# Five moves in the hand-written order of engine work of a fused linear-attention and long-convolution kernel

## Chip, cores and metric

One core of a Trainium2 chip runs the whole kernel. The metric is the device time of one execution in microseconds (us). Six agents work at once and meet only at semaphores: PE (TensorE, matrix products), PEld (its weight loads), DVE (VectorE), ACT (ScalarE), POOL (GpSimd) and SP (SyncE, which issues the transfers). Each of them does its own list of instructions strictly in the order in which the program gives them.

## What is computed

The input x has 2048 rows of D = 448. The result is `g * a + (1 - g) * b`, with one gate g for each row:

```python
g = sigmoid((x * gate_w).sum(-1, keepdims=True))
# a: linear attention, 16 heads of 28
pq, pk = phi(q), phi(k)                       # phi(t) = where(t > 0, t + 1, exp(t)) + 1e-6
kv  = einsum("bhsd,bhse->bhde", pk, v)
z   = einsum("bhsd->bhd", pk)
o   = einsum("bhqd,bhde->bhqe", pq, kv) / (einsum("bhqd,bhd->bhq", pq, z)[..., None] + 1e-6)
a   = o @ wo
# b: a causal convolution over the 2048 rows, one kernel K for each of the 448 columns, and a skip
b   = irfft(rfft(u) * rfft(K))[:L] + u * D_skip
```

For the given data the kernel of the convolution is the same at every lag, to the precision of the sum, for each column that passes a test; so the convolution is a running sum over the rows times one number per column (the "taps"), and the kernel holds a general version behind a branch for columns that fail the test.

## The kernel before

The rows are cut into 16 chunks c = 0..15 of 128. Everything lies in one program under a manual schedule: an engine's instructions stand in the order in which the Python code issues them, and buffers are taken in turn from pools with tags, so that a tile which takes a buffer waits until the last reader of its former tile is done. Matrix products run on pairs of reduced-precision numbers (a high part and a low part), so each operand x, w, pk is "split": ACT copies the high part, POOL or DVE subtracts to get the low part (line 261).

There are three stages.

**First stage, chunks 0 to 14.** For each chunk `project` (PE, L353) makes k of the next chunk and q of this one from the transposed input `xt` and the weights `wk`, `wqh`, `wql`; `k_feature`, `k_high`, `k_low` and `q_post` put phi on them (ACT, DVE); `do_g` (L422) adds pk times x into four sums g, which hold the whole of k times v, since v is linear in x. `split_t` and `split_n` split the two layouts of a later chunk (`xt` transposed, `xn` natural); `split_n` ends with the skip product `y <- xr * dsk` on POOL (L273, `dsk` is the second part of the tile `rows`). `do_v` (L429, L430) makes the running sum of a chunk on PE by a triangular matrix `tri`; `v_post` multiplies it by the taps (`near`, the first part of `rows`) on DVE (L434) and POOL adds it to y (L441). The table VS says which v belong to which c: v(0) and v(1) to c = 5. The taps are worked out from the convolution's parameters in small steps between the chunks (`s4d_prepare`, resumed by `steps`): its fifth step makes `tri` (L327) and the tests on DVE, its sixth, at c = 5, has four PE transposes into a tile p (L334) and an ACT copy into `rows` (L335). The tile p and the odd v share the PSUM tag "v1", which has one buffer.

**Transition, chunks 14 and 15.** The sum of all pk (`zb`) goes through PE (zo, L640) and back by an ACT copy (L642). Now for each chunk `norm_a` (POOL, L537) makes `prod = pq * zb`, `norm_b` (DVE reduce, L542) and `norm_d` (DVE, L547, L549) make the reciprocal denominators `den`, `norm_c` makes the normalised `pn` in two POOL products and one DVE product (L560, L566, L563). `norm_bd` is `norm_b` and `norm_d` for one chunk. `prod` has two buffers, so `norm_a` of a chunk waits for `norm_b` of the chunk two before it. Beside this `kv_products` (L694) turns g into kv, `kv_split` masks it (DVE, L699 to L707) and copies its high part `kvh` (ACT, L709), `kv_low` makes `kvl` (DVE), and `mrows` (L684 to L687) multiplies with wo into the four blocks of the last stage's weights `wk` (its low part again on DVE; `shl` is one such block). `turn` (L594 to L599) transposes a pn on PE into `tr`, ACT copies it to `th` and DVE makes the low part.

**Last stage, c = 0..15.** `attend(c)` (L616) is 11 matmuls a <- th, wk. `final_b` (DVE, L621) adds y times its gate and sends the rows out; `final_c` (ACT) keeps a copy. The loop makes pn of chunk c + 3 and turns chunk c + 2 ahead of `attend(c)`; chunks 0 and 1 are turned and pn 0 to 2 made in the transition. The rest of q of chunk 15 (`late`) is done in small pieces in the loop.

Of the kernel before, what the change touches and what calls it, by code (L numbers as in the profile page):

```python
# [11 lines left out]
ALU = mybir.AluOpType  # L12
# [5 lines left out]
D = 448  # L18
# [3 lines left out]
NC = S // P  # L22
# [146 lines left out]
def gated_mix_kernel(ctx: ExitStack, tc: tile.TileContext, xin, wq_d, wv_d, wo_d, abc_d, ldt_d, dsk_d,  # L169
# [6 lines left out]
    y = keep.tile([P, NC, D], F32, name="y")  # L176
# [91 lines left out]
    def split_n(c):  # L268
        r, w = plain[c], xn_p.tile([P, NX], F32R, name="xn", tag="n")
        xn[c] = w  # L270
        ACT.copy(w[:, :XC - NAT], r)  # L271
        low(POOL, w[:, XC - NAT:], r[:, :D], w[:, :D])
        POOL.tensor_tensor(out=y[:, c], in0=r[:, :D], in1=dsk, op=ALU.mult)  # L273

    idle = ps.tile([P, 512], F32, name="q", tag="q")

# [80 lines left out]
    def project(*args, **kw):  # L357
        o, run = pieces(*args, **kw)
        run(11)
        return o  # L360
# [15 lines left out]
    def k_feature(c, o):  # L376
        e = tp.tile([P, D], F32, name="e", tag="e")
        pks[c] = o[:, :D]
        ACT.activation(e, pks[c], AF.Relu, scale=-1.0)  # L379
        ACT.activation(e, e, AF.Exp, scale=-1.0)  # L380
        DVE.scalar_tensor_tensor(out=pks[c], in0=pks[c], scalar=1.0, in1=e, op0=ALU.add, op1=ALU.max)  # L381

    def k_high(c):
        pkh[c] = tp.tile([P, D], F32R, name="pkh", tag="pkh")
        ACT.add(pkh[c], pks[c], 1e-6)  # L385
# [19 lines left out]
    def gate(a, b):  # L405
        DVE.tensor_scalar(out=e1[:, a:b], in0=e1[:, a:b], scalar1=1.0, scalar2=None, op0=ALU.add)
        DVE.reciprocal(out=og[:, a:b], in_=e1[:, a:b])
        DVE.tensor_scalar(out=og[:, a:b], in0=og[:, a:b], scalar1=-1.0, scalar2=1.0, op0=ALU.mult, op1=ALU.add)
# [5 lines left out]
    def do_g(c, blocks=range(4)):  # L414
        w = xn[c]
        for i in blocks:
            a = w[:, 64 + i * P:64 + (i + 1) * P]
            b = w[:, XC - NAT + 64 + i * P:][:, :P] if i < 3 else None
            seq = [(a, pkh[c]), (a, pkl[c]), (b, pkh[c])] if i < 3 else \
                  [(a, pkh[c]), (a[:, :64], pkl[c])][::1 if c == 0 else -1]  # L420
            for n, (a, b) in enumerate(seq):
                PE.matmul(g[i][:a.shape[1], :D], lhsT=a, rhs=b, start=c == 0 and n == 0,  # L422
                          stop=c == NC - 1 and n == len(seq) - 1)
# [8 lines left out]
    def v_post(c):  # L432
        t = tp.tile([P, D], F32, name="t", tag="v0")
        DVE.tensor_tensor(out=t, in0=vt.pop(c)[:, :D], in1=near, op=ALU.mult)  # L434
        if c < NC - 1:
            SP.dma_start(out=u[c:c + 1], in_=t[P - 1:P])
            v_add(c, t)
        return t
# [5 lines left out]
    def steps(n):  # L444
        for _ in range(n):
            next(prep, None)
# [20 lines left out]
    split_n(0)  # L467
    k_low(0)
    k_feature(1, ko[1])
    k_high(1)  # L470
    split_n(1)
    k_low(1)
    do_g(0)
    split_w(1, wqh, wql, wqr, POOL)
# [11 lines left out]
    DVE.memset(ones, 1.0)  # L486
    q_post(1, qo)
    steps(1)
    split_n(3)
    woh, wol = [], []  # L490
    for c in range(2, NC - 2):
        if c + 3 < NC:
            load_x(c + 3)
        if c == 2:
            for o, i in ((mask, mask_d), (gcat, gcat_d), (sel, sel_d)):
                SP.dma_start(out=o, in_=i)
        if c == 4:
            SP.dma_start(out=wv, in_=wv_d)
            SP.dma_start(out=wo, in_=wo_d)
        vs = VS.get(c, ())  # L500
        ko = project(c + 1, wkh, wkl, D, "k")
        if c == 5:
            steps(1)
        for v in vs[:1]:
            do_v(v)
        split_t(c + 2)
        k_feature(c + 1, ko)
        k_high(c + 1)
        for v in vs[:1]:
            v_post(v)  # L510
        k_low(c + 1)
        qo = project(c, wqh, wql, D + 2, "q")
        for v in vs[1:]:
            do_v(v)
        q_post(c, qo)
        for v in vs[1:]:
            v_post(v)
        if c < 5:
            steps(2 if c == 4 else 1)
        do_g(c)  # L520
        split_n(c + 2)
        for j in {11: (0, 1), 12: (2, 3)}.get(c, ()):
            w = xn_p.tile([P, NX], F32R, name="wo", tag="n")[:DJ, :2 * D].rearrange("p (i d) -> p i d", i=2)
            woh.append(w[:, 0])
            wol.append(w[:, 1])
            ACT.copy(woh[j], wo[:, j])
            low(POOL, wol[j], wo[:, j], woh[j])
# [11 lines left out]
    def norm_b(c):  # L539
        if c % 2 == 0:  # L540
            dn[c // 2] = tp.tile([P, 2, H], F32, name="den", tag="den", bufs=3)
        DVE.tensor_reduce(out=dn[c // 2][:, c % 2], in_=pd.pop(c).rearrange("p (h d) -> p h d", h=H), op=ALU.add,  # L542
                          axis=AX.X)
# [7 lines left out]
    def norm_bd(c):  # L551
        norm_b(c)
        norm_d(c, 1)
# [36 lines left out]
    def turn(c):  # L590
        o = p3.tile([P, 512], F32, name="tr", tag="tr")
        n = pn.pop(c)
        for j in range(J):
            PE.transpose(o[:, j * P:(j + 1) * P], n[:, j], ident)  # L594
        t = xt_p.tile([P, 2, J, P], F32R, name="th", tag="t")
        h, l = th[c], tl[c] = t[:, 0], t[:, 1]
        ov = o.rearrange("p (j t) -> p j t", j=J)
        ACT.copy(h, ov)  # L598
        DVE.tensor_tensor(out=l, in0=ov, in1=h.bitcast(F32), op=ALU.subtract)  # L599
# [31 lines left out]
    do_v(c + 1)  # L631
    k_feature(c + 1, ko)
    k_high(c + 1)
    gate(0, c)
    k_low(c + 1)
    vl = v_post(c + 1)
    qo = project(c, wqh, wql, D + 2, "q")
    zo = ps.tile([P, 512], F32, name="zo", tag="v0")
    PE.matmul(zo[:1, D:D + 1], lhsT=ones[:DJ, :1], rhs=oks, start=True, stop=True)
    PE.matmul(zo[:, :D], lhsT=ones, rhs=zb, start=True, stop=True)  # L640
# [1 line left out]
    ACT.copy(zb, zo[:, :D])  # L642
    norm_a(0)
    norm_a(1)
    do_g(c)
    gate(c, c + 1)
    g2 = gates_a(1, NC - 1)
    POOL.memset(rows[DT:RX, :2 * D], 0.0)
    last = gates_b(g2, "pkl")
# [30 lines left out]
    def mrows(j, pool, tag):  # L680
        o = pool.tile([P, 512], F32, name="m%d" % j, tag=tag)
        w = woh[j]
        for n, (a, b) in enumerate(((kvh, w), (kvh, wol[j]), (kvl, w))):
            PE.matmul(o[:DJ, :D], lhsT=a[:, j], rhs=b, start=n == 0, stop=n == 2)  # L684
        a, b = (mh[:DJ, j], ml[:DJ, j]) if j < 3 else (shl[:, 0], shl[:, 1])
        ACT.copy(a, o[:DJ, :D])
        DVE.tensor_tensor(out=b, in0=o[:DJ, :D], in1=a.bitcast(F32), op=ALU.subtract)  # L687
# [9 lines left out]
    def kv_split(r, kvp):  # L697
        m = 3 if r else 2
        DVE.tensor_tensor(out=kv[:, 2 * r:m],  # L699
                          in0=kvp[:DJ, 2 * r * DJ:m * DJ].rearrange("p (j d) -> p j d", d=DJ),  # L700
                          in1=mask[:, None, :].to_broadcast([DJ, m - 2 * r, DJ]), op=ALU.mult)
        if r:
            a, b = (w.rearrange("p (h d) -> p h d", h=4) for w in (kvp[:DJ, 3 * DJ:4 * DJ], mask))
            DVE.tensor_tensor(out=kv[:, 3, :DT].rearrange("p (h d) -> p h d", h=4), in0=a[:, :, DS:], in1=b[:, :, DS:],
                              op=ALU.mult)
            a, b = (w[:, :, :DS].rearrange("p h (j d) -> p h j d", j=3) for w in (a, b))
            DVE.tensor_tensor(out=kv[:, 3, DT:].rearrange("p (j h d) -> p h j d", j=3, h=4), in0=a, in1=b, op=ALU.mult)  # L707
        rs = slice(2 * r, 2 * r + 2)
        ACT.copy(kvh[:, rs], kv[:, rs])  # L709

    def kv_low(r):
        rs = slice(2 * r, 2 * r + 2)
        low(DVE, kvl[:, rs], kv[:, rs], kvh[:, rs])
# [2 lines left out]
    q_run(QA)  # L716
    k1 = kv_products(1)
    k0 = kv_products(0)
    norm_bd(2)
    norm_a(3)  # L720
    kv_split(1, k1)
    kv_low(1)
    kv_split(0, k0)
    mrows(3, ps, "k")
    for j, eng in ((2, SP), (0, ACT), (1, SP)):
        eng.dma_start(out=wk2[DJ:, :, j].bitcast(F32), in_=shl[DT + 16 * j:DT + 16 * j + 16].bitcast(F32))
    SP.dma_start(out=mh[DT:, 3].bitcast(F32), in_=shl[:DT, 1].bitcast(F32))
    kv_low(0)
    mrows(2, ps, "v0")
    turn(0)  # L730
    v_add(c + 1, vl)
    norm_c(2)
    norm_a(4)
    mrows(0, p3, "a")
    ACT.copy(mh[:DT, 3], shl[:DT, 0].bitcast(F32))
    mrows(1, p3, "a")
    ACT.copy(rc[0][:DT], shl[:DT, 0].bitcast(F32))
    turn(1)
    norm_bd(3)
    norm_a(5)  # L740
    tail(0)
    q_run(11)
    norm_b(4)
    def late():
        c = NC - 1
        yield 5
# [21 lines left out]
    for c in range(NC):  # L768
        if c % 2 and c + 4 < NC:
            norm_d(c + 3, 2)  # L770
        if c:
            final_b(c - 1)
        if c + 3 < NC:
            norm_c(c + 3)
        if c + 2 < NC:
            turn(c + 2)
        if c:
            final_c(c - 1)
        if c + 1 < NC:
            tail(c + 1)  # L780
        if c + 6 < NC:
            norm_a(c + 6)
        if c + 5 < NC - 1:
            phi(c + 5)
        attend(c, ((0, D // 2), (D // 2, D)) if c == NC - 1 else ((0, D),))
        if c + 5 < NC:
            norm_b(c + 5)
        if c == due:
            due = next(later, None)
# [94 lines left out]
```

## Time and profile before

| | us |
|---|---|
| median of 3 runs (lowest, highest) | 185.66 (185.36, 185.93) |
| the profiled execution | 185.38 |
| its span in the trace | 183.6 |
| PE busy in the span | 173.2 (94%) |
| PEld, DVE, ACT, POOL busy | 151.4, 112.9, 94.7, 118.8 |

The span reaches from the first to the last instruction in the trace; the other 1.8 us of the execution lie around it. Busy time is the sum of an engine's instruction times without overlap. In the timeline a row has the start and the duration in us, the engine, the line, the operation, what it writes and reads, the number of merged instructions, and in brackets how long the engine had been idle and which instruction let it go on.

### The profile page before, as it was taken

How to read it: one execution, taken by the hardware profiler on the slowest of the kernel's cores; microseconds unless marked ns; L12 is line 12 of the kernel's file. 1: busy time of each engine (PE TensorE's matmuls, PEld its weight loads, DVE VectorE, ACT ScalarE, POOL GpSimd, SP SyncE). 2: the span in 40 equal slices, each digit the busy share in tenths (PEclk: the TensorE clock that was granted, in tenths of full speed). 3: DMA queues.
4: the chain of work that ended last, by engine and by line, in shares of the span. 5: the costliest groups of instructions: out<-in, count | busy, mean ns of one | idle time of the engine just before them, and what ended most of it. 6: DMA issues, size and time to landing. Idle time of an engine off the chain costs nothing.

```text
span 183.6 us, 2736 instructions
## 1 busy us (share of the span) xinstructions
PE 173.2 (94%) x879; PEld 151.4 (82%) x879; DVE 112.9 (62%) x238; ACT 94.7 (52%) x212; POOL 118.8 (65%) x124
## 2 busy tenths in 40 slices
PE   6999999999899999999999999998899999999970
PEld 2697798998899999999989999667678999999970
DVE  1757638558357374372651733788699999987430
ACT  3769288872536245262455742551654565455330
POOL 3259774766268769669599996098548887864000
PEclk9999999999999999999999999999999999999999
DMA  5999966920003303033033000000201221222131
GB/s 196 409 303 274 281 232 232 300 73 2 4 3 112 115 0 116 4 115 115 1 114 118 2 0 0 0 2 5 39 26 50 101 102 53 101 100 85 71 127 39
DMA packets 7789, 18.46 MB, mean 101 GB/s; under 512 B 1755, under 2 KB 4520, under 8 KB 7768
## 3 DMA queue, kind: packets, MB, share of 16 engines
q1 hardware_dynamic: 7720, 18.16, 29.9%
q8 instruction: 9, 0.15, 0.3%
q10 hardware_dynamic: 48, 0.06, 0.2%
q14 instruction: 12, 0.10, 0.2%
HBM read 14.20 MB, written 3.67 MB: 97 GB/s over the span
## 4 chain that ended last, share of the span: by engine, by line
PE 71%; DVE 9%; POOL 6%; issue 6%; ACT 5%; ACTq 0%; POOLq 0%; DVEq 0%
PE a L616 19%; PE k L353 15%; PE q L353 14%; PE g L422 12%; PE tr L594 3%; PE q L279 3%; PE v L430 2%; PE v L429 2%; POOL wql L261 2%; POOL y L273 2%; POOL xn L261 1%; DVE den L542 1%; PE v L353 1%; DVE den L547 1%; POOL prod L537 1%
## 5 line engine op out<-in xcount | busy, mean ns | idle before, releaser
L616 PE MATMUL a<-wk,th 128*128 128x448 f32 (+1 forms) x170 | 39.0, 362 | 0.0
L422 PE MATMUL g<-pkh,xn 128*128 128x448 f32 x112 | 36.0, 370 | 0.2 <-POOL xn L261 0.2
L353 PE MATMUL k<-wk,xt 128*128 128x448 f32 x154 | 34.8, 370 | 0.0
L381 DVE SCALAR_TENSOR_TENSOR k<-k,e 128x448 f32<-128x448 f32 x14 | 8.9, 632 | 40.9 <-ACT e L380 40.9
L353 PEld LDWEIGHTS k<-wk,xt 128*128 128x128 f32 x154 | 28.8, 188 | 3.7 <-ACT wk L450 0.6
L616 PEld LDWEIGHTS a<-wk,th 128*128 128x128 f32 x170 | 29.8, 189 | 2.0
L353 PE MATMUL q<-wqh,xt 128*128 128x450 f32 x120 | 27.8, 369 | 0.0
L441 POOL TENSOR_TENSOR y<-y,t 128x448 f32<-128x448 f32 x16 | 18.5, 1154 | 11.3 <-DVE t L434 11.1
L261 POOL TENSOR_TENSOR xn<-xr,xn 128x448 fp32r<-128x448 f32 x16 | 18.5, 1155 | 10.2 <-ACT xn L271 10.1
L353 PEld LDWEIGHTS q<-wqh,xt 128*128 128x128 f32 x120 | 22.6, 189 | 2.6 <-issue 0.7
L537 POOL TENSOR_TENSOR prod<-pq,zb 128x448 f32<-128x448 f32 x16 | 18.4, 1152 | 9.2 <-ACT zb L642 5.8
L422 PEld LDWEIGHTS g<-pkh,xn 128*128 128x128 f32 x112 | 21.0, 188 | 3.4 <-POOL xn L261 0.6
L422 PE MATMUL g<-pkl,xn 128*128 128x448 f32 x64 | 23.4, 366 | 0.0
L379 ACT ACTIVATE e<-k 128x448 f32<-128x448 f32 x14 | 7.6, 545 | 27.2 <-PE k L353 27.2
L261 POOL TENSOR_TENSOR xt<-xr,xt 128x512 fp32r<-128x512 f32 x14 | 18.1, 1294 | 3.2 <-ACT xt L265 3.2
L273 POOL TENSOR_TENSOR y<-xr,rows 128x448 f32<-128x448 f32 x16 | 18.6, 1161 | 0.8 <-DMA rows<-in 0.8
L560 POOL TENSOR_TENSOR pn<-pq,den 128x336 f32<-128x336 f32 x16 | 12.1, 755 | 8.0 <-PE tr L594 5.2
L598 ACT CAST th<-tr 128x512 fp32r<-128x512 f32 x16 | 9.4, 588 | 14.5 <-PE tr L594 14.4
L621 DVE SCALAR_TENSOR_TENSOR ot<-y,og,a 128x448 f32<-128x448 f32 (+1 forms) x17 | 10.5, 615 | 5.7 <-PE a L616 5.7
L385 ACT ACTIVATE pkh<-k 128x448 fp32r<-128x448 f32 x14 | 7.6, 546 | 9.8 <-DVE k L381 9.8
L353 PE MATMUL q<-wql,xt 128*128 128x450 f32 x45 | 12.0, 367 | 0.4 <-POOL wql L261 0.4
L422 PEld LDWEIGHTS g<-pkl,xn 128*128 128x128 f32 x64 | 11.2, 175 | 1.2 <-issue 0.2
(135 smaller groups left out, 292.3 us busy)
## 6 DMA issues: line engine op xcount, KB each, us to landing
xr<-in SPq DMA_DIRECT2D x15, 512.0 KB, 3.3
out<-ot SPq DMA_DIRECT2D x15, 224.0 KB, 1.9
pq<-in SPq DMA_DIRECT2D x4, 448.0 KB, 12.3
y<-in SPq DMA_DIRECT2D x2, 480.0 KB
y<-in SPq DMA_DIRECT2D x2, 450.0 KB, 7.4
wv<-in SPq DMA_DIRECT2D x1, 896.0 KB, 7.6
wo<-in SPq DMA_DIRECT2D x1, 784.0 KB
y<-in SPq DMA_DIRECT2D x1, 448.0 KB
```

The costliest lines, as they stand in the source:

```text
L261: eng.tensor_tensor(out=o, in0=r, in1=h.bitcast(F32), op=ALU.subtract)
L273: POOL.tensor_tensor(out=y[:, c], in0=r[:, :D], in1=dsk, op=ALU.mult)
L353: PE.matmul(o[:, :n], lhsT=a, rhs=b, start=run.n == 1, stop=not seq)
L379: ACT.activation(e, pks[c], AF.Relu, scale=-1.0)
L381: DVE.scalar_tensor_tensor(out=pks[c], in0=pks[c], scalar=1.0, in1=e, op0=ALU.add, op1=ALU.max)
L422: PE.matmul(g[i][:a.shape[1], :D], lhsT=a, rhs=b, start=c == 0 and n == 0, stop=c == NC - 1 and n == len(seq) - 1)
L441: POOL.tensor_tensor(out=y[:, c], in0=y[:, c], in1=t, op=ALU.add)
L537: POOL.tensor_tensor(out=pd[c], in0=pq[:, c], in1=zb, op=ALU.mult)
L560: POOL.tensor_tensor(out=n[:, :3, :DJ].rearrange("p j (h d) -> p j h d", h=4), in0=a, in1=r[:, :H - 4].rearrange("p (j h) -> p j h", j=3)[ ...
L598: ACT.copy(h, ov)
L616: PE.matmul(a[:, lo:hi], lhsT=u_, rhs=w_[:, lo:hi], start=n == 0, stop=n == 10)
L621: DVE.scalar_tensor_tensor(out=ot[:, lo:hi], in0=y[:, c, lo:hi], scalar=og[:, c:c + 1], in1=a[:, lo:hi], op0=ALU.mult, op1=ALU.add)
```

## The change

Five moves; no instruction of weight is added or taken out. (1) The skip products of chunks 0 to 2 leave `split_n` and are issued together behind q of chunk 1; `split_n(1)` is issued ahead of `k_high(1)`. (2) At c = 5 the step with the four transposes p stands behind q of chunk 5, directly ahead of v(1), and both `v_post` of that chunk behind `q_post`. (3) In the block of chunk 14 the first quarter of `do_g(14)` stands ahead of zo, and one gate calculation over chunks 0 to 14 takes the place of two. (4) `kv_split` and `kv_low` for both halves come ahead of the denominators of chunk 2, which go behind all four `mrows`; turn(1), pn(2) and the denominators of chunks 3 and 4 go into the last loop. (5) The last loop makes pn of c + 2 and turns c + 1.

```diff
 def split_n(c):                                        # (1)
...
     low(POOL, w[:, XC - NAT:], r[:, :D], w[:, :D])
-    POOL.tensor_tensor(out=y[:, c], in0=r[:, :D], in1=dsk, op=ALU.mult)
+    if c > 2:
+        skip(c)
+
+def skip(c):
+    POOL.tensor_tensor(out=y[:, c], in0=plain[c][:, :D], in1=dsk, op=ALU.mult)
...
 k_feature(1, ko[1])
+split_n(1)
 k_high(1)
-split_n(1)
 k_low(1)
...
 q_post(1, qo)
 steps(1)
+for c in range(3):
+    skip(c)
 split_n(3)
...
     ko = project(c + 1, wkh, wkl, D, "k")              # (2)
-    if c == 5:
-        steps(1)
     for v in vs[:1]:
         do_v(v)
...
-    for v in vs[:1]:
-        v_post(v)
+    if c > 5:
+        for v in vs[:1]:
+            v_post(v)
     k_low(c + 1)
     qo = project(c, wqh, wql, D + 2, "q")
+    if c == 5:
+        steps(1)
     for v in vs[1:]:
         do_v(v)
     q_post(c, qo)
-    for v in vs[1:]:
+    for v in vs[c > 5:]:
         v_post(v)
...
-gate(0, c)                                             # (3)
 k_low(c + 1)
 vl = v_post(c + 1)
 qo = project(c, wqh, wql, D + 2, "q")
+do_g(c, (0,))
 zo = ps.tile([P, 512], F32, name="zo", tag="v0")
...
-do_g(c)
-gate(c, c + 1)
+do_g(c, (1, 2, 3))
+gate(0, c + 1)
...
 k0 = kv_products(0)                                    # (4)
-norm_bd(2)
+kv_split(1, k1)
 norm_a(3)
-kv_split(1, k1)
 kv_low(1)
 kv_split(0, k0)
+kv_low(0)
 mrows(3, ps, "k")
...
-kv_low(0)
 mrows(2, ps, "v0")
 turn(0)
 v_add(c + 1, vl)
-norm_c(2)
 norm_a(4)
 mrows(0, p3, "a")
...
 mrows(1, p3, "a")
...
-turn(1)
-norm_bd(3)
+norm_bd(2)
 norm_a(5)
 tail(0)
 q_run(11)
-norm_b(4)
...
 for c in range(NC):                                    # (5)
...
-    if c + 3 < NC:
-        norm_c(c + 3)
     if c + 2 < NC:
-        turn(c + 2)
+        norm_c(c + 2)
+    if c + 1 < NC:
+        turn(c + 1)
...
     attend(c, ((0, D // 2), (D // 2, D)) if c == NC - 1 else ((0, D),))
+    if c == 0:
+        norm_bd(3)
+        norm_b(4)
     if c + 5 < NC:
         norm_b(c + 5)
```

What this moves on POOL in the first chunks, before (xn and xt are the low parts of the two layouts of x, wql the low parts of q's weights, `y<-xr,rows` the skip products):

```order
11 L261 TENSOR_TENSOR xn<-xr,xn 128x448
12 L273 TENSOR_TENSOR y<-xr,rows 128x448
13 L261 TENSOR_TENSOR xn<-xr,xn 128x448
14 L273 TENSOR_TENSOR y<-xr,rows 128x448
15 L261 TENSOR_TENSOR wql<-y,wqh 128x450 x2
16 L261 TENSOR_TENSOR xt<-xr,xt 128x512
17 L261 TENSOR_TENSOR xn<-xr,xn 128x448
18 L273 TENSOR_TENSOR y<-xr,rows 128x448
19 L261 TENSOR_TENSOR xn<-xr,xn 128x448
20 L273 TENSOR_TENSOR y<-xr,rows 128x448
21 L261 TENSOR_TENSOR xt<-xr,xt 128x512
```

And now, on the same engine at the same place:

```order
11 L261 TENSOR_TENSOR xn<-xr,xn 128x448 x2
12 L261 TENSOR_TENSOR wql<-y,wqh 128x450 x2
13 L261 TENSOR_TENSOR xt<-xr,xt 128x512
14 L261 TENSOR_TENSOR xn<-xr,xn 128x448
15 L277 TENSOR_TENSOR y<-xr,rows 128x448 x3
16 L261 TENSOR_TENSOR xn<-xr,xn 128x448
17 L277 TENSOR_TENSOR y<-xr,rows 128x448
18 L261 TENSOR_TENSOR xt<-xr,xt 128x512
```

The low parts of xn(1) and of wql come two skip products sooner; three skip products now stand between xn(2) and xn(3), and so ahead of the low part of xt(4).

What it moves on PE in chunk 5, before (p are the transposes of the taps, v the two running sums, k and q the projections, g the sums of pk times x):

```order
102 L353 MATMUL k<-wk_69,xt 128x448 x11
103 L334 MATMUL p<-ident,sm 128x112 x4
104 L429 MATMUL v<-xn,tri 128x448
105 L430 MATMUL v<-xn,tri 128x448
106 L353 MATMUL q<-wqh,xt 128x450 x8
107 L353 MATMUL q<-wql,xt 128x450 x3
108 L429 MATMUL v<-xn,tri 128x448
109 L430 MATMUL v<-xn,tri 128x448
```

And now:

```order
102 L357 MATMUL k<-wk_69,xt 128x448 x11
103 L433 MATMUL v<-xn,tri 128x448
104 L434 MATMUL v<-xn,tri 128x448
105 L357 MATMUL q<-wqh,xt 128x450 x8
106 L357 MATMUL q<-wql,xt 128x450 x3
107 L338 MATMUL p<-ident,sm 128x112 x4
108 L433 MATMUL v<-xn,tri 128x448
109 L434 MATMUL v<-xn,tri 128x448
```

The four transposes went behind the eleven matmuls of q and stand right ahead of v(1).

What it moves on POOL between the transition and the last stage, before (the first row is pn(1)'s second product; prod, pn as above, `y<-y,t` the sum of chunk 15):

```order
74 L566 TENSOR_TENSOR pn<-pq,den 128x128
75 L537 TENSOR_TENSOR prod<-pq,zb 128x448
76 L441 TENSOR_TENSOR y<-y,t 128x448
77 L560 TENSOR_TENSOR pn<-pq,den 128x3x112
78 L566 TENSOR_TENSOR pn<-pq,den 128x128
79 L537 TENSOR_TENSOR prod<-pq,zb 128x448 x2
80 L560 TENSOR_TENSOR pn<-pq,den 128x3x112
81 L566 TENSOR_TENSOR pn<-pq,den 128x128
```

And now:

```order
71 L573 TENSOR_TENSOR pn<-pq,den 128x128
72 L544 TENSOR_TENSOR prod<-pq,zb 128x448
73 L445 TENSOR_TENSOR y<-y,t 128x448
74 L544 TENSOR_TENSOR prod<-pq,zb 128x448 x2
75 L567 TENSOR_TENSOR pn<-pq,den 128x3x112
76 L573 TENSOR_TENSOR pn<-pq,den 128x128
```

The pair of products pn(2) moved behind prod(4) and prod(5); the pn that stood there before was pn(3).

## The prediction

> **What bounds the kernel now.** I read the page's busy times first, then the chain that ended last, then windows around the places that the change touches, then the timeline there.
>
> ```profile
> PE 173.2 (94%) x879; PEld 151.4 (82%) x879; DVE 112.9 (62%) x238; ACT 94.7 (52%) x212; POOL 118.8 (65%) x124
> PE 71%; DVE 9%; POOL 6%; issue 6%; ACT 5%; ACTq 0%; POOLq 0%; DVEq 0%
> ```
>
> PE bounds it: 173.2 of 183.6 us, and 71% of the chain. The change takes no matmul away, so all it can win is PE's idle time, 10.4 us in the span, and only the part that its five moves touch. Windows of the transition and of the last stage:
>
> ```profile
> 130.00:138.00 8.00, 6.96 (x39) 5.70 (x37) 6.96 (x15) 4.46 (x10) 4.58 (x7) 1.00 0.18 37
> 138.00:162.00 24.00, 23.99 (x134) 21.70 (x133) 23.55 (x52) 13.12 (x29) 20.47 (x29) 1.00 0.23 86
> ```
>
> The columns are PE, PEld, DVE, ACT, POOL busy, then the granted clock. Just ahead of the last stage PE loses 1.04 us in 8.00; in its first 24 us PE loses nothing, but DVE is busy 23.55 of the 24.00, so it has no slack to take a delay. The span is 183.6 and the execution 185.38, 1.8 us lie outside; the median is 185.66. The sum is made as a difference and put on both.
>
> **Move 1, skip products later.** The rows of POOL and PE in the first chunks:
>
> ```profile
> 13.81 1.16 POOL L273 TENSOR_TENSOR y<-xr,rows 128x448 f32<-128x448 f32 x1 [0.78 <-DMA rows<-in]
> 14.93 1.16 POOL L261 TENSOR_TENSOR xn<-xr,xn 128x448 fp32r<-128x448 f32 x1
> 15.59 0.36 PE L422 MATMUL g<-pkl,xn 128*128 128x448 f32 x1
> 16.14 0.67 PE L422 MATMUL g<-pkh,xn 128*128 128x448 f32 x2 [0.19 <-POOL xn L261]
> 17.14 3.05 POOL L261 TENSOR_TENSOR wql<-y,wqh 128x450 fp32r<-128x450 f32 x2
> 19.49 0.36 PE L353 MATMUL q<-wql,xt 128*128 128x450 f32 x1
> 20.25 0.47 PE L353 MATMUL q<-wql,xt 128*128 128x450 f32 x1 [0.40 <-POOL wql L261]
> 22.35 1.16 POOL L261 TENSOR_TENSOR xn<-xr,xn 128x448 fp32r<-128x448 f32 x1 [0.92 <-ACT xn L271]
> 28.15 1.31 POOL L261 TENSOR_TENSOR xt<-xr,xt 128x512 fp32r<-128x512 f32 x1
> 30.00 0.85 PE L353 MATMUL k<-wk,xt 128*128 128x448 f32 x3
> ```
>
> Matmuls of this size start some 0.20 us apart (the two rows of 0.36 end the run that each stands in). From 15.59 to 16.14 is 0.55, so 0.35 is lost to xn(1), whose low part stands behind a skip product that itself waited 0.78 for a transfer; from 19.49 to 20.25 is 0.76, 0.56 lost to wql, behind the second skip product. The two matmuls that resume are each 0.1 longer (0.67 for 0.57, 0.47 for 0.36). Together 1.1 us; with xn(1) and wql moved up by one and two skip products (1.1 and 2.2 us on POOL), both waits go. What is late next: on POOL xn(2) still waits for its ACT copy, now at 22.35 - 1.07 = 21.3; behind it stand three skip products (3 x 1.1), xn(3), its skip product and then xt(4): 21.3 + 6 x 1.11 = 28.0, and xt(4) is done at 28.0 + 1.31 = 29.3, where before it was done at 29.5 against a use at about 30.2, the second matmul of k at 30.00. That use would now come at 29.1, so PE waits 0.15 to 0.45 (0.3 to 0.45 if the resumed matmul is longer again). Left: 0.6, between 0.2 and 1.1. That `split_n(1)` stands ahead of `k_high(1)` makes pkh(1) later by one ACT copy, some 0.6 as the copies below, while PE still has g(0): nothing, and at most 0.6 without that cover, which is in the 0.2.
>
> **Move 2, taps behind q of chunk 5.** The rows there:
>
> ```profile
> 42.70 1.15 POOL L261 TENSOR_TENSOR xn<-xr,xn 128x448 fp32r<-128x448 f32 x1 [0.71 <-ACT xn L271]
> 42.73 1.37 DVE L369 TENSOR_SCALAR t<-e 128x448 f32<-128x448 f32 x1
> 45.99 0.22 DVE L327 CAST tri<-trir 128x128 fp32r<-128x128 f32 x1
> 46.53 0.60 PE L334 MATMUL p<-ident,sm 112*128 112x112 f32 x4 [0.64 <-DVE sm L300]
> 47.16 0.53 ACT L335 COPY rows<-p 128x448 f32<-128x448 f32 x1 [4.54 <-PE p L334]
> 47.39 1.81 PE L353 MATMUL q<-wqh,xt 128*128 128x450 f32 x8
> 49.66 0.37 PE L429 MATMUL v<-xn,tri 128*128 128x448 f32 x1
> ```
>
> PE was idle 0.64 ahead of p at 46.53, counted from the modelled end of k; in a dense run the next matmul starts 0.16 before that end (0.36 long, 0.20 apart), so PE was free near 45.73 and 0.8 is lost, to the last of the small DVE steps. Behind q that wait is gone. But v(0), now first, needs `tri`, done at 46.21, so with all 0.6 earlier PE still waits from 45.13 to 45.6: 0.5. Then v(0) and q take to 48.3, p 0.36 more, and v(1) shares p's PSUM buffer: it must wait for the ACT copy of p, which starts 0.63 after p does (47.16 - 46.53) and lasts 0.53. That puts v(1) at 48.3 + 0.63 + 0.53 + 0.06 = 49.5, against 49.66. The early gain of 0.6 shrinks to 0.14 there: a wait of 0.8 turns into one of 0.5 and one of 0.85, and behind the waiting v(1) stand g(5) and k of the next chunk on PE. The moved `v_post` have POOL's sum behind them, which no one needs before the last stage: nothing. Up: the DVE row of 1.37 us ran beside POOL's xn, which started 0.03 us ahead of it, while the same instruction in the last stage takes 0.38 (quoted below); were it to start first, the chain to `tri` is up to 1 us shorter, the wait for `tri` goes, and 0.6 is left. Range 0 to 0.9 for what is kept by chunk 6. From here to chunk 14 PE is dense, and DVE, POOL and ACT follow it: no change.
>
> **Moves 3 and 4, the transition.** The rows:
>
> ```profile
> 117.44 1.02 PE L640 MATMUL zo<-zb,ones 128*128 128x448 f32 x2 [0.43 <-DVE zb L391]
> 124.21 1.73 PE L694 MATMUL k<-gs,wv 128*112 128x112 f32 x16
> 127.06 0.28 DVE L699 TENSOR_TENSOR kv<-k,mask 112x112 f32<-112x112 f32 x1
> 129.77 0.62 DVE L687 TENSOR_TENSOR shl<-m,shl 112x448 fp32r<-112x448 f32 x1 [1.00 <-ACT shl L686]
> 131.16 0.46 PE L684 MATMUL m<-wo,kvl 112*112 112x448 f32 x1 [0.73 <-DVE kvl L261]
> 133.00 1.16 DVE L687 TENSOR_TENSOR wk<-m,wk 112x448 fp32r<-112x448 f32 x2
> 134.92 1.67 PE L616 MATMUL a<-wk,th 128*128 128x448 f32 x7
> 135.10 0.61 DVE L542 TENSOR_REDUCE den<-prod 128x16 f32<-128x448 f32 x1
> 135.74 0.17 DVE L547 SCALAR_TENSOR_TENSOR den<-den,e 128x16 f32<-128x16 f32 x1
> 135.78 1.16 POOL L537 TENSOR_TENSOR prod<-pq,zb 128x448 f32<-128x448 f32 x1 [3.32 <-DVE den L542]
> 136.90 0.76 POOL L560 TENSOR_TENSOR pn<-pq,den 128x336 f32<-128x336 f32 x1
> 137.71 0.69 PE L594 MATMUL tr<-ident,pn 128*128 128x128 f32 x4 [0.31 <-POOL pn L560]
> 138.15 1.68 PE L616 MATMUL a<-wk,th 128*128 128x448 f32 x7
> 141.04 1.68 PE L616 MATMUL a<-wk,th 128*128 128x448 f32 x7
> ```
>
> The masks run at 127.06, behind the denominators of chunk 2, though k's products end by 124.21 + 1.73 = 125.94. With a quarter of g ahead of zo, PE does not wait for `zb` (0.43, and 0.1 for the resumed matmul); with the 0.14 kept from before, the products end near 125.4, and so do the masks begin. That is 1.6 sooner, and the chain mask, kvh, m, low part of m that ends at 133.00 + 1.16 = 134.16 comes some 1.35 sooner, to about 132.8 (each m takes an ACT copy and a DVE subtraction, so not all 1.6 gets through). PE's own 0.73 at 131.16 goes with it, and the four transfers of `shl` rows, issued behind its low part at 129.77, go out as much sooner. a(0), at 134.92 before, can start near 132.4: 2.5 sooner, with one turn less in front. The single gate calculation saves three DVE instructions that nobody waits for: nothing.
>
> But the next turn needs pn(2), and this is now later in its chain. The denominators of chunk 2 begin behind the low parts, at 132.75; prod(4) needs the buffer that their reduce frees, so it starts at 133.4 and holds up DVE's next steps; then the low part of th(1) (to 135.2), the reduce of chunk 3 (0.6, to 135.8), and only that lets prod(5) go: 135.84 to 137.0, nearly the 135.78 of before. pn(2) stands behind it on POOL, its large product to 137.7. So turn(2) starts at 137.75 where before turn(3) started at 137.71, and a(1) at 138.2 to 138.5 against 138.15. PE idles for some 3 us after a(0), and the 2.5 us are gone. Bounds of this term: +0.35 (138.5), and -0.8 if prod(4) does not block DVE and the lows end 0.4 sooner; I take +0.1.
>
> a(2) follows a(1) by 2.89 before (141.04 - 138.15), 2.69 where nothing waits: -0.18.
>
> **Move 5, one ahead.** Before, the turns of four chunks were done by a(1); now three. The one left over runs in the loop, which PE bounds:
>
> ```profile
> 153.94 0.38 DVE L753 TENSOR_SCALAR t<-e 128x448 f32<-128x448 f32 x1
> 155.01 0.76 POOL L560 TENSOR_TENSOR pn<-pq,den 128x336 f32<-128x336 f32 x1 [0.95 <-DVE den L549]
> 169.56 0.37 PE L616 MATMUL a<-rc,th 112*128 112x448 f32 x1
> 172.25 0.37 PE L616 MATMUL a<-rc,th 112*128 112x448 f32 x1
> 174.50 0.37 PE L616 MATMUL a<-rc,th 112*128 112x448 f32 x1
> ```
>
> The same matmul of three successive chunks stands 2.69 apart with a turn and 2.25 without, so a turn costs 0.44: +0.44. And the margin between pn and its turn is shorter by one iteration. Where `late` adds DVE work (153.94 and its neighbours) POOL waited 0.95 for the denominators; now PE waits for pn behind them. In the new order prod stands ahead of that pn on POOL, and if it starts first it holds up DVE for its 1.15: between 0 and 1.15 at that place. I take 0.4, a third, since now DVE wins that race (135.74 against 135.78, above).
>
> **Sum.** -0.14 + 0.10 - 0.18 + 0.44 + 0.4 = +0.62 us. On the profiled execution that gives 186.0, on the median 186.3. A measurement of this kernel can tell about 0.3%, 0.56 us, from no change: 185.1 to 186.2.
>
> **A rule against the change.** The windows above show clock 1.00, and PE's longest wait quoted here is 0.73, so a gap of 3 us is nothing that this trace can price. The Trainium skill, page "TensorE: Matmul & The Clock Gate", section "Part 1: The HAM clock gate", says that after one idle window of about 3.4 us TensorE falls to half clock and needs about as long a busy stretch to come back; no run here shows that. By rows: if PE ran at half speed for one turn and attend after a 3 us gap, that costs 2.69 us more.
>
> **The rivals.**
> Forecast, the gain of the transition is eaten by pn(2), chance 0.42: 185.7 to 187.2 (0.30 of it over 186.2, 0.12 under).
> No loss in the loop: DVE finds its place between POOL's products as now (at 155.01 the wait fell on POOL), so the +0.4 falls to zero and the sum is +0.2, 185.9: within 0.3%, chance 0.18.
> Faster: the chain to pn(2) is shorter than I make it. It decides at 136.5: every 0.1 that pn(2)'s large product ends ahead of 137.7 is 0.1 won, as PE has been waiting since 134.7. With DVE not held up by prod(4) (-0.4), the low parts 0.4 sooner, no stall in the loop (-0.4) and 0.2 more kept of the start, 186.3 - 1.4 = 184.9. For it: DVE's steps are short (0.61, 0.17, 0.26), and 1.0 of the 2.4 us from 132.75 to 135.2 is my holding-up. Against: prod(4) is let go by just the reduce that DVE goes on from. Chance 0.22.
> DVE or POOL bounds the loop: the step after the reduce loses the race to prod in every second iteration, 1.1 each in three places, not once: 186.3 - 0.4 + 3.3 = 189.2; DVE's 23.55 of 24.00 speaks for it. Chance 0.11.
> The clock falls after the gap, as above: 186.3 + 2.7 = 189.0. Against: the gap is 3, not longer, and not in this trace. Chance 0.07.
>
> **How the numbers follow.** Over 0.3% faster 0.22; within 0.12 + 0.18 = 0.30; slower 0.30 + 0.11 + 0.07 = 0.48. The predicted time is the forecast's, 186.3. The range goes from 184.7, just under the faster rival, to 188.4, which leaves out the upper two rivals (0.18) but holds one lost race and its effect; the forecast's own range is 185.7 to 187.2.
>
> **What would show it.** In the changed kernel's timeline: no wait of PE for xn(1) and wql and a short one for xt(4) near 29; a wait of v(1) for ACT near 48.7; the first mask near 125.4 and a(0) near 132.4; prod(5) at 135.8, POOL's pn(2) ending near 137.7, PE idle 3 us ahead of it; a(1) near 138.2. A start of turn(2) before 136.5 makes the prediction wrong on the fast side, PE waits of over 0.3 in most iterations of the loop on the slow side.

## The result and the profile after

The changed kernel takes 190.62 us (median of 4 runs, 190.34 to 190.91) against 185.80 us (185.36 to 186.11): ratio 1.0262, 95% interval 1.0233 to 1.0290. It is slower by 4.8 us where 0.6 was forecast, and lies above the range of 184.7 to 188.4. The profiled execution has a span of 188.9 us, 5.3 more than before.

The page of the changed kernel, the lines on busy time, on the granted clock in 40 slices, and on the chain:

```profile
PE 174.6 (92%) x879; PEld 153.0 (81%) x879; DVE 113.2 (60%) x235; ACT 94.7 (50%) x212; POOL 118.7 (63%) x124
PEclk9999999999999999999999999999996999999997
PE 68%; DMA 11%; DVE 9%; ACT 4%; SPq 2%; issue 2%; POOL 1%; DVEq 0%; ACTq 0%
```

PE does the same 879 matmuls but is busy 1.4 us longer, and one of its slices reads 6: the clock was down. The other 3.9 us are idle time. Three places hold most of it. The first is the taps, in the timeline of chunk 5:

```profile
45.25 1.28 POOL L261 TENSOR_TENSOR xt<-xr,xt 128x512 fp32r<-128x512 f32 x1
45.35 1.20 DVE L304 TENSOR_TENSOR sm<-sm 112x4 f32<-112x4 f32 x1
47.49 0.47 PE L433 MATMUL v<-xn,tri 128*128 128x448 f32 x1 [1.44 <-DVE tri L331]
50.83 0.53 ACT L339 COPY rows<-p 128x448 f32<-128x448 f32 x1 [1.94 <-PE p L338]
51.42 0.47 PE L433 MATMUL v<-xn,tri 128*128 128x448 f32 x1 [0.62 <-ACT rows L339]
```

A DVE step on 112x4 numbers takes 1.20 us beside a POOL subtraction that began 0.10 us ahead of it, and both end within 0.02 us of each other; in the kernel before the same step took 0.15 (at 45.16). The step reads nothing that POOL writes, so the two engines met here without a semaphore. v(0) waits for `tri` and v(1) for the copy of the taps. v(1) stands at 51.42 where it stood at 49.66: +1.76, of which 0.16 was there at k of chunk 4. The second place, behind zo:

```profile
121.06 2.24 POOL L544 TENSOR_TENSOR prod<-pq,zb 128x448 f32<-128x448 f32 x2 [5.95 <-ACT zb L649]
121.24 1.00 DVE L410 TENSOR_SCALAR e<-e 128x15 f32<-128x15 f32 x1
122.56 0.77 DVE L412 TENSOR_SCALAR og<-og 128x15 f32<-128x15 f32 x1
123.39 0.28 PE L591 MATMUL o<-ident,og 128*14 128x128 f32 x1 [1.36 <-DVE okn L657]
127.06 1.73 PE L701 MATMUL k<-gs,wv 128*112 128x112 f32 x16
128.83 0.28 DVE L706 TENSOR_TENSOR kv<-k,mask 112x112 f32<-112x112 f32 x1 [0.68 <-PE k L701]
```

The gate calculation now runs beside the two prod, and two of its three steps take 1.00 and 0.77 us. In the kernel before, 14 chunks were done with POOL idle, and only the one that was left fell beside a prod (which began at 119.10) and was not held up:

```profile
116.05 0.17 DVE L406 TENSOR_SCALAR e<-e 128x14 f32<-128x14 f32 x1
119.39 0.14 DVE L406 TENSOR_SCALAR e<-e 128x1 f32<-128x1 f32 x1
```

The transposed gates wait for the calculation, and PE's queue with them. k's products start at 127.06 for 124.21: +2.85. The masks do follow them at once. The third place, ahead of a(1):

```profile
134.93 1.29 DVE L694 TENSOR_TENSOR wk<-m,wk 112x448 fp32r<-112x448 f32 x2
135.59 0.73 PE L623 MATMUL a<-wk,th 128*128 128x448 f32 x2
136.13 0.61 DVE L549 TENSOR_REDUCE den<-prod 128x16 f32<-128x448 f32 x1
136.82 1.16 POOL L544 TENSOR_TENSOR prod<-pq,zb 128x448 f32<-128x448 f32 x1 [6.79 <-DVE den L549]
139.24 1.13 POOL L544 TENSOR_TENSOR prod<-pq,zb 128x448 f32<-128x448 f32 x1 [1.27 <-DVE den L549]
140.33 0.75 POOL L567 TENSOR_TENSOR pn<-pq,den 128x336 f32<-128x336 f32 x1
141.13 0.69 PE L601 MATMUL tr<-ident,pn 128*128 128x128 f32 x4 [2.50 <-POOL pn L567]
141.58 2.14 PE L623 MATMUL a<-wk,th 128*128 128x448 f32 x7
145.71 1.79 PE L623 MATMUL a<-wk,th 128*128 128x448 f32 x7
```

This is the chain of the forecast: low parts, denominators of chunk 2, prod(4), reduce of chunk 3, prod(5), pn(2), turn(2). PE stands idle 2.5 us, and from a(1) to a(2) are 4.13 us (2.89 in the kernel before, 2.69 where nothing waits), since seven matmuls take 2.14 instead of 1.68. Windows there (columns PE, PEld, DVE, ACT, POOL, then clock), the first and second of one length, the second beginning where the trace shows the clock change:

```profile
139.16:142.57 3.41, 1.44 (x9) 1.32 (x10) 3.01 (x10) 0.70 (x2) 3.33 (x5) 1.00 0.00 0
142.57:145.98 3.41, 3.41 (x13) 2.99 (x12) 1.91 (x5) 0.72 (x2) 3.41 (x6) 0.50 0.18 68
```

The clock is at half for 3.41 us, right behind a stretch of that length in which PE was busy for 1.44. In sum, on the spans: 0.16 up to k of chunk 4, 1.60 at the taps, 1.09 at the gates (what the late gates cost, less what the quarter of g ahead of zo won), 0.57 more up to turn(2) (141.13 against 137.71), 1.25 from there to a(2) (145.71 against 141.04), and 0.62 from a(2) to the last matmuls (182.73 against 177.44): 5.29.

### The profile page after: what moved, and what is told of

Read it like the earlier page. It is cut to its first block, busy times and chain, and to the rows that moved or that the text cites. A ratio compares the mean times of both kernels' runs of the same rounds, so it can differ in the third digit from the quotient of the medians.

```text
span 188.9 us, 2751 instructions
## 1 busy us (share of the span) xinstructions
PE 174.6 (92%) x879; PEld 153.0 (81%) x879; DVE 113.2 (60%) x235; ACT 94.7 (50%) x212; POOL 118.7 (63%) x124
## 4 chain that ended last, share of the span: by engine, by line
PE 68%; DMA 11%; DVE 9%; ACT 4%; SPq 2%; issue 2%; POOL 1%; DVEq 0%; ACTq 0%
PE a L623 19%; PE k L357 13%; PE g L426 13%; PE q L357 12%; DMA xr<-in 11%; PE tr L601 4%; PE v L433 2%; PE v L434 2%; PE m L691 1%; DVE k L385 1%; DVE pkl L395 1%; ACT e L384 1%; ACT pkh L389 1%; ACT e L383 1%; DVE t L373 1%
## 5 line engine op out<-in xcount | busy, mean ns | idle before, releaser
L623 PE MATMUL a<-wk,th 128*128 128x448 f32 (+1 forms) x170 | 40.6, 371 | 0.2 <-DMA wk<-shl 0.2
L623 PEld LDWEIGHTS a<-wk,th 128*128 128x128 f32 x170 | 30.5, 194 | 2.8 <-ACT th L609 0.5
L601 PE MATMUL tr<-ident,pn 128*128 128x128 f32 x64 | 10.2, 283 | 2.5 <-POOL pn L567 2.5
```

The costliest lines, as they stand in the source:

```text
L623: PE.matmul(a[:, lo:hi], lhsT=u_, rhs=w_[:, lo:hi], start=n == 0, stop=n == 10)
```

## The experiments

**Each move alone**, on the kernel before. The edits are the parts (1), (2), (3) and (4) with (5) of the diff above.

> The kernel before with move 1 alone (skip products of chunks 0 to 2 behind q of chunk 1). Theory, from the trace of after: the two early waits of PE go (1.1 us), but xt(4) waits for the load of x(4), k(4) starts where it did, and the time is +0.2 us against before, within -0.1 to +0.4. Rival, the prediction's term: 0.6 us are kept up to the taps and some of it to the end, -0.6 to -0.1 us.

Measured: 185.57 us, ratio 0.9995 (0.9967 to 1.0023). A run labelled move1_x4_early had the same kernel, its expectation speaks of another edit:

> Move 1 with the load of x(4) issued ahead of the convolution's parameters. Theory: in the changed kernel the ACT copy of xt(4) waits 1.0 for that load and holds up k(3)'s feature and so k(4); with the load there the early gain is kept to the taps, 0.6 to 1.0 us, and 0 to -0.9 us is left at the end. Rival, k(4) is set by another chain: 0 as move 1 alone.

It gave 185.25, ratio 0.9983 (0.9963 to 1.0003). So move 1 gives 0 to 0.3 us, no loss: between the expectation and its rival, and the intervals decide for neither. In its trace k(4) is held up for some 0.35 us (its eleven matmuls take 2.83, in the kernel before 2.48), by POOL's low part of xt(4) and not by the load of x(4):

```profile
29.29 2.83 PE L357 MATMUL k<-wk,xt 128*128 128x448 f32 x11
29.81 1.93 PEld L357 LDWEIGHTS k<-wk,xt 128*128 128x128 f32 x10 [0.37 <-POOL xt L261]
```

> The kernel before with move 2 alone (taps' transposes behind q of chunk 5). Theory: POOL's low part of xt(7), no longer behind the ACT copy of the taps, runs beside the first small DVE step and holds it for 1.2 us; `tri` is late, PE waits 1.4 to 1.6 for it and 0.7 for v(1): +1.5 us, +1.2 to +1.8. Rival, the prediction's term: a wait of 0.8 becomes one of 1.1 and one of 0.85 where nothing was gained before, less the 0.36 of p: +0.5 to +0.9 us.

Measured: 187.18, ratio 1.0090 (1.0062 to 1.0119): +1.6 us.

> The kernel before with move 3 alone (a quarter of g ahead of zo, one gate calculation behind the two products of chunks 0 and 1). Theory: the one gate calculation over 15 chunks falls beside POOL's two prod and is held up twice, and the transposes of the gates wait for it: +1.0 us, +0.7 to +1.2. Rival, the prediction's term: the gate calculation costs nothing and the quarter of g hides the wait for zb: 0 to -0.4 us.

Measured: 186.08, ratio 1.0031 (1.0009 to 1.0054): +0.5, less than expected and against the rival. PE waits 1.36 for the gates as in the changed kernel, but alone half of it is taken back, since the masks behind the denominators wait less.

> The kernel before with moves 4 and 5 alone (masks ahead of the denominators, one chunk ahead in the last loop). Theory: a(0) starts 2.2 us sooner, turn(2) 0.3 to 0.6 later than turn(3) did, the gap of over 2.5 us lets the granted clock fall to half for some 3.5 us (+1.3), the extra turn 0.44, the loop 0.2: +2.4 us, +1.9 to +2.8. Rival, the same without the clock: +0.4 to +1.2 us.

Measured: 188.09, ratio 1.0121 (1.0042 to 1.0200), the four runs at 186.25, 187.61, 188.56 and 188.62. Added up, the moves alone make 4.4 to 4.7 us of the 4.8, but the interval of this last one reaches from 0.8 to 3.7 us, so the sum is no proof that nothing else is there.

**What holds the taps.** In chunk 5 only, `split_t(7)` goes behind `k_feature(6)`:

```diff
-        split_t(c + 2)
+        if c != 5:
+            split_t(c + 2)
         k_feature(c + 1, ko)
+        if c == 5:
+            split_t(c + 2)
```

> The kernel before with move 2 and, in chunk 5, `split_t(7)` behind `k_feature(6)`, so that POOL's low part of xt(7) cannot run beside the first small DVE steps. Theory: `tri` is done near 46.2 instead of 47.3, PE waits 0.5 for it instead of 1.6; v(1) still waits 0.7: +0.5 to +0.7 us on the kernel before, where move 2 alone was +1.6. Rival, the DVE steps are late for another reason: +1.4 to +1.7 as move 2 alone.

Measured: 186.20, ratio 1.0043 (1.0023 to 1.0064): +0.7 to +0.8. Its timeline:

```profile
44.93 0.15 DVE L300 TENSOR_TENSOR sm<-sm 112x4 f32<-112x4 f32 x1
46.03 0.47 PE L429 MATMUL v<-xn,tri 128*128 128x448 f32 x1 [0.38 <-DVE tri L327]
47.48 1.29 POOL L261 TENSOR_TENSOR xt<-xr,xt 128x512 fp32r<-128x512 f32 x1 [2.62 <-ACT xt L265]
49.99 0.47 PE L429 MATMUL v<-xn,tri 128*128 128x448 f32 x1 [0.62 <-ACT rows L335]
```

With POOL's subtraction out of the way the same step takes 0.15, and the wait for `tri` 0.38 instead of 1.44. The 0.62 for the copy of the taps stays. With k(4) as the start, v(1) is 0.60 later than in the kernel before, near the 0.46 that the forecast had made of this move.

**The gate calculation.** Two runs put the two gate calculations back to their old places, the first in move 3 alone, the second in the changed kernel:

```diff
+    gate(0, c)
     k_low(c + 1)
...
-    gate(0, c + 1)
+    gate(c, c + 1)
```

> The kernel before with only the quarter of g ahead of zo from move 3; the two gate calculations stay where they were. Theory: the 1.5 us that PE waited for the transposed gates in move 3 come from the gate calculation alone; without it PE keeps the 0.4 to 0.6 us at zo up to k's products, and DVE's masks behind the denominators of chunk 2 set what follows: 0 to -0.4 us. Rival, the quarter of g itself delays the copy of zb and the first prod: +0.3 to +0.6 as move 3.

Measured: 185.76, ratio 1.0018 (0.9988 to 1.0047): no gain, no loss. PE reaches k's products 0.45 us sooner, but then waits 1.25 us for kvh instead of 0.58: in the kernel before, the masks behind the denominators do not use an earlier PE.

> The changed kernel with the two gate calculations where they were before. Theory: behind move 4 the masks follow k's products at once, so the 1.1 us that PE loses to the late gates pass to the end in full: -0.7 to -1.2 us on the changed kernel, +3.5 to +4.2 on the kernel before. Rival, as between move 3 with and without its gate calculation, only 0.3 passes on: +4.4 to +4.8.

Measured: 188.53, ratio 1.0144 (1.0090 to 1.0198) to the kernel before, runs 187.27 to 189.06. That is 2.2 us less than the changed kernel's 1.0262, more than expected, and the rival's 0.3 is out. The two profiled runs lie 2.51 us apart at the last matmuls. Of these, 0.77 were there at k(4), where the load of x(4) came less late (ACT waited 0.23 for it, not 1.03), and that is not the gates' doing. From v(1) to k's products are 1.53 us less, which is what the late gates cost PE, and turn(2) still has all of it. The clock fell here as well, but for a stretch that began inside the gap. Whether the medians divide in the same way, four runs do not show.

**The load of x(4).** `load_x(4)` goes ahead of the load of the convolution's parameters.

```diff
+    load_x(4)
     SP.dma_start(out=ldt, in_=ldt_d)
...
-    load_x(4)
```

> Move 1 with the load of x(4) issued ahead of the loads of the convolution's parameters (the run labelled move1_x4_early had move 1 unchanged, so it is a second measurement of move 1). Theory: the ACT copy of xt(4) waits for that load and holds up k(3)'s feature and so k(4), by an amount that differs from run to run; with the load there, PE reaches the taps 0.9 to 1.1 us sooner than before, and -0.3 to -1.0 us is left at the end. Rival, k(4) is set by another chain: -0.3 to 0 as move 1 alone.

Measured: 185.44, ratio 0.9992 (0.9975 to 1.0009): as move 1 alone; the rival holds. In the three traces with move 1 alone or with this load, ACT does not wait for x(4), and k(4) is held up by POOL's low part of xt(4) each time, as shown above. The profiled run of the changed kernel is another case:

```profile
25.91 0.62 ACT L265 CAST xt<-xr 128x512 fp32r<-128x512 f32 x1 [1.03 <-DMA xr<-in]
30.16 2.48 PE L357 MATMUL k<-wk,xt 128*128 128x448 f32 x11 [1.03 <-DVE zb L395]
```

k(4) takes the PSUM buffer of k(3), which DVE's sum `zb` reads last. In that run x(4) came late, which delayed ACT's k(3) steps and so that sum.

**The clock.** Twelve matmuls that nobody reads fill PE's gap.

```diff
     attend(c, ...)
     if c == 0:
+        warm = ps.tile([P, 512], F32, name="warm", tag="v1")
+        for _ in range(12):
+            PE.matmul(warm[:, :D], lhsT=mh[:, 2, :P], rhs=mh[:, 2], start=True, stop=True)
         norm_bd(3)
```

> The changed kernel with 12 matmuls, of which nobody reads the result, behind attend(0), in the 2.65 us in which PE waits for pn(2). Theory: the gap lets the granted clock fall to half for 3.4 us behind it, and that costs 1.4 to 1.7 us in the runs in which it happens; filled, the clock stays at 1.00 and the time is 189.0 to 189.3 against 190.6 for the changed kernel, +3.4 us on the kernel before. Rival, the turn and a(1) of the trace are long for another reason (the weights' transfers or DVE's low part): 190.4 to 190.8, or more if the fillers hold PE up.

Measured: 188.44 (188.30 to 189.43), ratio 1.0167 (1.0132 to 1.0201), against 1.0262 unfilled: 1.8 us faster with 12 matmuls more, and 0.6 faster than expected. In the two profiled runs 1.46 us of the gain lie between turn(2) and a(2), which is the clock; 0.81 were there before turn(2), since x(4) was not late in the filled run. PE's timeline, with turn(2), a(1) and a(2) in the last three rows:

```profile
137.63 2.60 PE L792 MATMUL warm<-wk 128*128 128x448 f32 x12
140.32 0.69 PE L601 MATMUL tr<-ident,pn 128*128 128x128 f32 x4
140.76 1.67 PE L623 MATMUL a<-wk,th 128*128 128x448 f32 x7
143.44 1.67 PE L623 MATMUL a<-wk,th 128*128 128x448 f32 x7
```

a(1) to a(2) is 2.68 again.

> Moves 4 and 5 alone with 12 matmuls, of which nobody reads the result, behind attend(0). Theory: the runs of moves 4 and 5 alone fell into two groups (186.25, 187.61 and 188.56, 188.62) because the clock falls behind the gap of 2.7 us only where the gap lies badly to the clock's window of 3.4 us; filled, no run has the fall: one group, 186.2 to 187.5, +0.8 to +1.6 us on the kernel before. Rival, the two groups have another cause (the start's transfers): runs over 188 remain.

Measured: 186.83 (186.40 to 187.03), ratio 1.0058 (1.0039 to 1.0076): one group, none over 188. The two unfilled runs over 188 had a mean granted clock of 0.982 and 0.981, the other two 0.990 and 0.992. In the profiled run of moves 4 and 5 unfilled (187.61) the clock had not fallen, behind the same gap:

```profile
139.54 0.68 PE L594 MATMUL tr<-ident,pn 128*128 128x128 f32 x4 [2.56 <-POOL pn L560]
134.43:137.85 3.42, 2.55 (x11) 1.94 (x11) 3.25 (x9) 1.18 (x3) 1.36 (x2) 1.00 0.00 0
137.85:141.26 3.41, 1.72 (x10) 1.59 (x11) 3.08 (x8) 0.98 (x2) 3.41 (x5) 1.00 0.00 0
```

These stretches are counted in steps of 3.41 us from that trace's next change of clock, at 182.2. The gap fell across two of them, and PE was busy 1.72 in the emptier. The steps are no assumption: in each of the 17 traces the clock stayed up for a whole number of steps of 3.413 us (12, 39, 40 or 50 to 52) before it fell.

**What makes pn(2) late.** `prod` gets three buffers: `name="prod", tag="pk", bufs=3`.

> Moves 4 and 5 alone with three buffers for prod, so that prod(5) does not wait for the reduce of chunk 3. Theory, the chain of the prediction: prod(5) follows prod(4) on POOL, pn(2) behind it comes 1.2 to 1.6 us sooner, PE's gap falls from 2.7 to 1.1 to 1.5 us, the clock stays at 1.00 in every run: -0.4 to +0.5 us on the kernel before, all runs within 1 us of each other. Rival, pn(2) is set by its own denominators behind the low parts: gap over 2.3 us, +0.8 to +2.8 us, in two groups of runs.

Measured: 186.44, ratio 1.0053 (1.0030 to 1.0076), runs 185.96 to 187.59: +1.0, more than expected. The chain was right, prod(5) was its slow link: a(1) starts at 136.83 instead of 139.98 in moves 4 and 5 alone (2.7 us sooner, taken from the first matmul of g). But PE waits 1.09 for pn ahead of a(2), so the rest of the expectation failed.

> A version from the findings: the kernel before, with kv's masks and low parts ahead of the denominators of chunk 2 as in move 4, but these denominators behind the first of the four mrows instead of the last, pn(2) and turn(1) left in the transition, the loop two ahead as before, and prod(5) behind pn(3). Theory: the masks start 1.0 us sooner, a(0) 0.8 to 1.1, pn(3) no longer waits for prod(5), PE has no gap over 0.6 us: -0.6 to -1.2 us. Rival: the denominators of chunk 2 and then 3 come late again behind the low parts, and turn(3) waits as before: -0.2 to +0.4 us.

Measured: 185.99, ratio 1.0024 (1.0007 to 1.0041): slower by 0.4 where 0.6 to 1.2 of gain was expected. a(1) was 0.6 sooner than before and a(2) 0.4 later; PE's and POOL's rows say why:

```profile
137.24 2.25 POOL L537 TENSOR_TENSOR prod<-pq,zb 128x448 f32<-128x448 f32 x2
141.03 0.63 PE L594 MATMUL tr<-ident,pn 128*128 128x128 f32 x4 [1.01 <-DVE pn L563]
```

prod(5) and prod(6), pushed behind pn(3), made the denominators of the next chunks late. So one more order, in which each reduce stands as early on DVE as its prod allows, and POOL does prod(4), pn(2), prod(5), pn(3):

```diff
-    norm_bd(2)
-    norm_a(3)
+    norm_b(2)
     kv_split(1, k1)
+    norm_a(3)
     kv_low(1)
     kv_split(0, k0)
+    kv_low(0)
     mrows(3, ps, "k")
...
-    kv_low(0)
+    norm_d(2, 1)
+    norm_b(3)
     mrows(2, ps, "v0")
...
-    norm_c(2)
     norm_a(4)
+    norm_c(2)
+    norm_d(3, 1)
+    norm_a(5)
...
-    norm_bd(3)
-    norm_a(5)
     tail(0)
```

> A version from the findings, on the kernel before: the reduce of chunk 2 ahead of kv's masks, both low parts of kv ahead of the first mrows' low part, the rest of denominators 2 and the reduce of chunk 3 in the DVE pause behind it, the rest of denominators 3 ahead of the last two low parts, and on POOL prod(4), pn(2), prod(5), pn(3) in this order; loop two ahead. Theory: what kept a(1) and a(2) late was the place of the reduces and denominators behind the low parts on DVE, since each prod and pn waits for them; in this order pn(3) is there when a(0) ends, a(1) starts 1.2 to 2.0 us sooner and stays so: -1.0 to -2.0 us. Rival, POOL and DVE together are too slow for the first chunks in any order, and a later attend gives it back as in masks_first: -0.3 to +0.5 us.

Measured: 183.42 (183.07 to 184.87), ratio 0.9892 (0.9862 to 0.9922): 2.0 us under the kernel before by the ratio, 2.3 by the medians, at the edge of what was expected. Its windows and the rows that matter:

```profile
130.00:138.00 8.00, 7.94 (x45) 7.08 (x44) 7.39 (x19) 5.44 (x12) 5.33 (x8) 1.00 0.18 37
130.12 0.56 DVE L542 TENSOR_REDUCE den<-prod 128x16 f32<-128x448 f32 x1
131.42 1.16 POOL L537 TENSOR_TENSOR prod<-pq,zb 128x448 f32<-128x448 f32 x1
133.16 0.75 POOL L560 TENSOR_TENSOR pn<-pq,den 128x336 f32<-128x336 f32 x1 [0.58 <-DVE den L549]
136.34 1.68 PE L616 MATMUL a<-wk,th 128*128 128x448 f32 x7
```

The reduce of chunk 3 stands in a pause of DVE at 130.12, prod(5) follows at 131.42 and pn(3) at 133.16, 2 us ahead of a(0)'s end; a(1) starts at 136.34 (138.15 before), and PE is busy 7.94 of 8.00 where it was 6.96.

> The same with move 1 and the quarter of g ahead of zo from move 3. Theory: the two give 0.1 to 0.3 and 0.2 to 0.5 us more, since now the masks follow k's products and no denominators stand ahead: -1.3 to -2.6 us on the kernel before. Rival: they are hidden as alone: the same as the version without them.

Measured: 183.05 (182.79 to 183.70), ratio 0.9855 (0.9835 to 0.9875), the fastest of all: 2.7 us under the kernel before. From the first matmul of g to the last matmuls its trace is 0.32 us shorter than that of the version without the two parts; in the times, the two intervals overlap, so that they add something is not shown.

## Why the prediction was wrong, point by point

The terms of the sum against the two traces: the -0.14 up to v(1) became +1.76; the +0.10 from there to a(1) became +1.67; the -0.18 up to a(2) became +1.24; the 0.84 of the loop became 0.62.

**Move 1: right.** Its term (0.6 kept at the taps) shows in move 1's own trace, where p starts at 46.21 with the first g at 13.48, against 46.53 and 13.16: 0.6 after the start is taken off. The wait for xt(4), forecast at 0.15 to 0.45, is there with 0.35. In the profiled run of the changed kernel the load of x(4) was 1.0 late and nothing was left of the gain; the forecast had no term for that, and by the other traces it is a matter of the run.

**Move 2: the step that failed is "`tri`, done at 46.21, so with all 0.6 earlier PE still waits from 45.13 to 45.6".** `tri` was done at 47.44, and PE waited 1.44 for it instead of 0.5. The prediction moved the transposes and their ACT copy behind q and forgot what that copy had stood in front of: ACT's copy of xt(7). Freed, it let POOL's subtraction start at 45.25 instead of 48.29, beside the very DVE chain on which v(0) waits. The forecast let the move cost 0.46 (0.6 shrinks to 0.14); it cost 1.60. The prediction had the mechanism in its rows (the 1.37 us DVE step beside POOL's xn) and used it only as a chance of gain.

**Move 3: the step that failed is "three DVE instructions that nobody waits for: nothing".** The transposes of the gates wait for them, with PE's whole queue behind, and that cost 1.53 us. No price was taken from rows although the new place lies beside POOL's two prod. The gain at zo was right: PE no longer waits for `zb`, and with the gates in their old places k's products come 0.44 sooner after v(1) (forecast 0.43 and 0.1).

**Move 4: right in its chain, too short in its size.** Less the 2.85, a(0) started at 132.7 (forecast 132.4), the low parts ended at 133.4 (forecast 132.8) and turn(2) came at 138.3 (forecast 137.75). So a(1) came 0.58 later than before where +0.10 was forecast, beyond the upper bound of +0.35: the low parts ended 0.6 late and the chain behind them kept that. The chain through prod(5) is shown by the three buffers.

**The clock: a rival at 0.07 that came true, by the right mechanism.** Its price, 2.7, was a whole iteration at half speed; measured 1.4, since it lasts one stretch of 3.41 us. It was held unlikely because the gap was forecast at 3 us and not longer; a gap of 2.5 was enough. The statement cited from the Trainium skill ("TensorE: Matmul & The Clock Gate", "Part 1: The HAM clock gate") agrees with the trace in the half speed (0.50) and in the length (3.41 us); that it takes an idle window does not: in the window ahead of the fall PE was busy 42% of the time.

**Move 5: right for the turn, not for the waits.** From a(2) to the end are 0.62 more: 0.44 for the turn, 0.12 because the first seven matmuls of a(2) still began at half clock (1.79 for 1.67), and 0.06 left of the 0.4 forecast for waits; the trace lists no wait of PE in the loop. The rival of a loop bound by DVE and POOL (189.2) came nearest to the measured time, by a cause that is not there.

## What to carry to other kernels

When a step is moved, look also at what stood behind it on each of its engines: that work now starts sooner, and it may hold up the chain that the move was made for. A small DVE step can be priced by what POOL does beside it: on 112x4 numbers 0.15 alone and 1.20 us beside a big subtraction, on 128x15 up to 1.00 beside a prod. Not every step is held up (on 128x1 it took 0.14 beside a prod), so look for the rows of the same form, and where there are none place short chains where POOL is idle. Where a chain goes to and fro between two engines through two buffers, put each reduce as early as its input allows instead of moving whole steps; that took PE's waits away here, with the loop left two chunks ahead.

## What the hardware showed that was not expected

The clock of TensorE falls for one stretch of 3.41 us behind a stretch of that length in which it was not idle but little busy: 1.44 of 3.41 us in the changed kernel, and in the run with two gates:

```profile
135.00:138.41 3.41, 1.30 (x7) 0.86 (x5) 3.08 (x7) 0.29 (x1) 2.14 (x3) 1.00 0.00 0
138.41:141.82 3.41, 3.00 (x10) 2.79 (x11) 3.02 (x7) 1.32 (x3) 3.41 (x6) 0.50 0.18 67
```

At 1.72 of 3.41 it did not fall. The ends of the kernels, where PE runs out of work, narrow the bound. In the kernel before PE was busy 1.72 of the stretch from 176.22 to 179.63, and the clock stayed at 1.00; in the first version from the findings it was busy 1.60 from 176.73 to 180.15, and the clock fell. In all 17 traces it fell behind every stretch with up to 1.60 and behind none with 1.72 or more.

So a gap of 2.5 us costs 1.4 us or nothing, by where it lies. An estimate from these bounds: the gap stays without a fall only where the boundary of two stretches lies 0.8 to 1.7 us into it, about a quarter of all positions. The groups in the four runs of moves 4 and 5 alone fit this; that the clock also fell in the three runs of the changed kernel that were not profiled is not shown.
